# Moving weight and input loads between queues and visits in a fused attention and MLP kernel

## The chip, the cores and the metric

The kernel runs on one core of one Trainium2 chip. The metric is the device time of one execution in microseconds (us). Three timed runs of the kernel before took 363.74, 364.76 and 366.37 us; their median is 364.76. One further execution was taken with a profile.

## The reference, cut to what matters

One transformer block over 2048 tokens of width 576, in bfloat16, with a sliding, dilated attention (32 heads of 18, eight taps two tokens apart) and an MLP of width 4608:

```python
def A(x):                                   # x already normalised
    q, k, v = split(x @ wqkv)               # wqkv: 576 x 1728
    # token s sees s, s-2, ..., s-14 of its own head
    logits = einsum("bhsd,bhswd->bhsw", q, k[idx]) * 18 ** -0.5
    o = einsum("bhsw,bhswd->bhsd", softmax(masked(logits)), v[idx])
    return o @ wo                           # wo: 576 x 576
def B(y):
    return gelu(y @ w1 + b1) @ w2 + b2      # w1: 576 x 4608, w2: 4608 x 576
h   = x + A(layernorm(x))
out = h + B(layernorm(h))
```

## The kernel before

**Tiles.** Token `p * 16 + j` lies on partition `p` of tile `j`, so there are 16 tiles of 128 tokens. The taps of an even tile are even tiles. Even and odd tiles form two rings, and attention goes through each ring from the top down (`ATT_ORDER`); A[0] and A[1] below are its first two tiles, 14 and 12. A tap that would fall below tile 0 is a tile of the partition above. So, after a tile is done, its K or V slot in the ring is replaced by the same rows moved down one partition: `store_halo` writes K and V to DRAM (`kv_dram`), and `halo` reads them back shifted (`kv_ring<-kv_dram`).

**First stage.** TensorE (PE) computes Q, K and V in 24 visits, each of two products of one tile with one of the three weight blocks; a visit takes about 2.5 us. Visits 0 to 11 are for the even tiles, 12 to 23 for the odd ones, two tiles (three visits) at a time. The contraction of 576 rows is four blocks of 128 (`wq_sb`) and a tail of 64, held twice, once for each half of the array (`wqh_sb`, loaded in two parts r). Even tiles are turned by PE (`tr_x`). Odd tiles are normalised on ScalarE (ACT), stored to DRAM (`out_x`, `xd<-q_all`) and read back turned by a DMA transpose (`in_x`, `xnT<-xd`), two tiles in one transpose; the first is wanted at visit 12, the third at visit 18.

Between these visits VectorE (DVE) works through LN statistics of all tiles and the attention of A[0] and A[1]: product of K and Q (L340), sums (L349), softmax, product with V (L395), sums (L401, L402). The product of A[1] with V needs the V halo of A[0]. PE then turns A[1]'s result (`tr_o`, `o_pt`) into PSUM tile "D", which the addition of x (`ln2_h`, L459) of A[0] has to free first. Wo is first used at visit 17. `add_b2` (L501) adds b2, loaded by SP at visit 14, to A[0]'s sum.

**The MLP** follows in eight groups of two tiles: w1 is read as six column pieces of 768 KB in order (`load_w1(0)` to `load_w1(5)`), w2 in seven.

**What sets the order.** It is written out by hand: the text between `manual_schedule` and the loop, and the tables `after`, `between`, `hooks` and `loads`, which say what is issued after which visit. Each engine executes its instructions in that order. Loads go out on SP unless an engine is named, and SP takes them strictly in order: an issue that waits holds all behind it. Each weight load issued in the visits also waits for the last PSUM read-out of its visit (`pace`). [...]

Of the kernel before, what the change touches and what calls it, by code (L numbers as in the profile page):

```python
# [17 lines left out]
def kernel(  # L18
# [12 lines left out]
    nc = tc.nc  # L31
    P = 128
    _, S, D = A_x.shape
# [12 lines left out]
    HP = P // 2  # L46
# [7 lines left out]
    EVEN, ODD = QKV_ORDER[:NT // 2], QKV_ORDER[NT // 2:]  # L54
# [3 lines left out]
    x3 = A_x.rearrange("b (p j) d -> p (b j) d", j=NT)  # L58
# [12 lines left out]
    x_all = wpool.tile([P, NT, D], BF16, name="x_all")  # L71
# [18 lines left out]
    wqh_sb = qp.tile([P, 3, D], BF16, name="wqh_sb")  # L90
# [9 lines left out]

    pace = [None]

    def load(out, in_):
        ins = nc.sync.dma_start(out=out, in_=in_).ins
        if pace[0] is not None:
            tc.add_manual_dep(ins, pace[0].name, sync_dep, reason="pace of the weight loads")

    def load_x(js):
        j0, n, step = js[0], len(js), 2
        load(x_all[:, j0:j0 + step * (n - 1) + 1:step, :], x3[:, j0:j0 + step * (n - 1) + 1:step, :])  # L110

    def load_wqkv(t, k0=0, k1=KF):
        load(wq_sb[:, k0:k1, t * D:(t + 1) * D],
             A_wqkv[k0 * P:k1 * P, t * D:(t + 1) * D].rearrange("(k p) c -> p k c", p=P))

    def load_wqkv_half(engine, t0, t1, r):
        n = D if r else HALF
        engine.dma_start(out=wqh_sb[half_rows(r), t0:t1, 0:n],
                         in_=A_wqkv[D - P + r * HP:D - HP + r * HP, t0 * D:t1 * D].rearrange("p (t c) -> p t c", c=D)[:, :, 0:n])

    def load_wo(qs):
        src = A_wo.rearrange("(h d) c -> h d c", h=H)
        for q in qs:
            load(wo_sb[q * H:(q + 1) * H, :, :], src[:, q:4 * KF:4, :])
            load(woh_sb[q * H:(q + 1) * H, :], src[:, 4 * KF + q % 2, q // 2 * HALF:(q // 2 + 1) * HALF])
# [82 lines left out]
    def half_rows(r):  # L208
        return slice(r * HP, (r + 1) * HP)
# [468 lines left out]
    def c_(fn, *a):  # L678
        return lambda: fn(*a)
# [99 lines left out]

    with tc.manual_schedule(engines={ENG.PE, ENG.Activation, ENG.DVE, ENG.SP, ENG.Pool}):  # L780
        load_x(EVEN[0:1])
        load_x(EVEN[1:2])
        for r in range(2):
            load_wqkv_half(nc.scalar, 1, 3, r)
        load_wqkv(1, 0, 2)
        load_wqkv(1, 2, KF)
        load_x(EVEN[2:3])
        load_wqkv(2, 0, 2)
        load_wqkv(2, 2, KF)
# [5 lines left out]
        load_wqkv(0, 0, 2)  # L795
        load_wqkv(0, 2, KF)
        for r in range(2):
            load_wqkv_half(nc.sync, 0, 1, r)
        nc.vector.memset(prod[:, 0:2, :], 0.0)
        nc.sync.dma_start(out=kv_dram[:, 0, :, :], in_=prod[0:NT, 0:2, :])  # L800
        load_w1h()
# [2 lines left out]
        for n in [512] * 8 + [P] * 5:  # L804
            nc.tensor.matmul(busy[:, 0, 0:n], lhsT=ones[:, 0:P], rhs=ones[:, 0:n], start=True, stop=True)
        nc.gpsimd.memset(mhalf[:], -0.5)
        nc.gpsimd.memset(eps2[:], EPS * EPS)
        make_identity(nc, ident[:])
        ln1_groups = [EVEN[0:1], EVEN[1:2], EVEN[2:3], EVEN[3:4], EVEN[4:5], EVEN[5:6],
                      EVEN[6:7], EVEN[7:8], ODD[0:4], ODD[4:6], ODD[6:8]]  # L810
        ln1 = {}
# [93 lines left out]
            ln2_send(d)  # L905
            ln2_ins(c, d)

        loads = {v: [c_(load_w1, c)] for c, v in enumerate((2, 3, 11, 13, 15, 17))}
        loads[4] = [c_(load_wo, range(4))]
        for n, v in enumerate((19, 19, 20, 20, 21, 22)):  # L910
            loads[v] = loads.get(v, []) + [c_(load_w2, n)]
        after = {
# [84 lines left out]
        p, q, r, s = "ABDC"  # L997

        gelu_table()
        for k, g in enumerate(GROUPS):  # L1000
            c, d = GROUPS[k + 1] if k + 1 < len(GROUPS) else (None, None)
# [87 lines left out]
            if 3 <= k < 7:  # L1089
                mlp2_fast(g, rows, (s, p, q, r), wo, x, True)  # L1090
                p, q, r, s = q, r, p, s
            else:
                mlp2_fast(g, rows, (q, p, r, s), wo, x)
                p, q, r, s = r, s, p, q
# [30 lines left out]
```

## Time and profile before

| | us |
|---|---|
| timed runs, median (lowest, highest) | 364.76 (363.74, 366.37) |
| profiled execution: its time | 363.39 |
| profiled execution: its span | 361.6 |
| PE busy in the span | 354.1 |
| DVE busy | 296.1 |
| ACT busy | 234.6 |
| GpSimd (POOL) busy | 46.5 |
| share of 16 transfer engines, ordinary queue | 43.6% |
| granted TensorE clock | 0.999 |

A line of a timeline is start, length, engine and line, operation, tiles, count, and in brackets the idle time of the engine before it and what ended it. A line of the chain of waits is start, length and what the end of the kernel went back to; "DMA" there is the time from issue to landing. [...] SPq, ACTq and POOLq are issues by these engines' sequencers. The names `w_sb` and `b_sb` are `w1_sb` and `b1_sb`: the profile leaves numbers out.

### The profile page before, as it was taken

Reading aid. Unit: us, or ns where it says so; the run is one execution under the profiler, and the core shown is the slowest. Engines: PE = TensorE matmul, PEld = TensorE weight load, DVE = VectorE, ACT = ScalarE, POOL = GpSimd, SP = SyncE. Lnnn points to the kernel's source line nnn. Section 1 sums busy time; section 2 is a strip of 40 time slices with the busy share of each in tenths; the row PEclk is TensorE's granted clock in tenths of the full one; section 3 lists DMA queues with packets and bytes.
Section 4 is the critical chain, followed back from the end, with each engine's and each line's share of the span. In section 5 each row is a group of like instructions: output and inputs, shape, how many; then the busy total and the mean of one; then the engine's idle time right before and its main releaser. Section 6 shows DMA issues by size and latency. Waiting matters only on the chain.

```text
span 361.6 us, 11550 instructions
## 1 busy us (share of the span) xinstructions
PE 354.1 (98%) x4942; PEld 295.1 (82%) x4942; DVE 296.1 (82%) x414; ACT 234.6 (65%) x519; POOL 46.5 (13%) x61
## 2 busy tenths in 40 slices
PE   8999999999999999999999999999999999999996
PEld 4778977887779977887788778877887788779974
DVE  5999989999989998997799899989998997520431
ACT  3879755897646783668656956695669566606620
POOL 2241004000112020201110202021102100201000
PEclk9999999999999999999999999999999999999999
DMA  8976699972546595732464555444545254343001
GB/s 244 322 249 192 189 269 274 377 248 64 149 87 105 172 206 95 129 78 51 82 111 106 66 125 84 106 83 107 86 106 83 62 84 70 51 106 51 4 1 34
DMA packets 62916, 46.18 MB, mean 128 GB/s; under 512 B 32192, under 2 KB 60608, under 8 KB 62864
## 3 DMA queue, kind: packets, MB, share of 16 engines
q1 hardware_dynamic: 58896, 41.39, 43.6%
q0 software_dynamic: 3744, 3.84, 9.8%
q8 instruction: 38, 0.62, 0.8%
q10 hardware_dynamic: 224, 0.22, 0.3%
q14 instruction: 14, 0.11, 0.1%
HBM read 23.27 MB, written 12.42 MB: 99 GB/s over the span
## 4 chain that ended last, share of the span: by engine, by line
PE 64%; DVE 21%; DMA 7%; ACT 3%; issue 2%; SPq 2%; POOL 0%; POOLq 0%; DVEq 0%; ACTq 0%
PE pm L218 34%; PE po L666 21%; PE po L578 5%; DVE prod L349 4%; DVE prod L340 3%; PE pw L218 3%; DVE prod L395 3%; DVE ln_stats L150 3%; ACT h_all L559 2%; DVE prod L401 2%; DMA td<-hn 2%; DMA hnT<-td 2%; DMA kv_ring<-kv_dram 1%; DMA x_all<-in_A_x_dram 1%; PE pq L218 1%
## 5 line engine op out<-in xcount | busy, mean ns | idle before, releaser
L218 PE MATMUL pm<-hnT,w_sb 64*128 64x256 bf16 x2304 | 143.0, 269 | 1.0 <-DMA hnT<-td 1.0
L559 ACT ACTIVATE h_all<-pm,b_sb 128x256 f16<-128x256 f32 (+1 forms) x288 | 108.4, 495 | 52.2 <-PE pm L218 51.6
L218 PEld LDWEIGHTS <-w_sb 64*128 64x128 bf16 x2304 | 115.2, 94 | 12.8 <-issue 2.7
L666 PEld LDWEIGHTS <-h_all 128*128 128x128 f16 x480 | 46.2, 98 | 13.7 <-issue 1.6
L218 PE MATMUL pq<-wq_sb,xnT 64*128 64x288 bf16 x720 | 55.6, 287 | 0.8 <-ACT xnT L269 0.3
L218 PEld LDWEIGHTS <-xnT 64*128 64x128 bf16 x864 | 44.5, 95 | 10.0 <-ACT xnT L269 0.7
L349 DVE TENSOR_TENSOR prod<-prod 128x2304 bf16<-128x2304 bf16 (+1 forms) x64 | 44.2, 691 | 2.0
L340 DVE TENSOR_TENSOR prod<-kv_ring,q_all 128x4608 bf16<-128x4608 bf16 x16 | 40.9, 2555 | 3.2 <-POOL ln_rstd L479 2.4
L395 DVE TENSOR_TENSOR prod<-kv_ring,probs 128x4608 bf16<-128x4608 bf16 x16 | 40.9, 2558 | 1.6 <-DMA kv_ring<-kv_dram 1.0
L218 PE MATMUL pm<-hnT,w1h_sb 64*128 64x256 bf16 x288 | 39.8, 269 | 0.0
L666 PE MATMUL po<-w2a_sb,h_all 128*128 128x288 bf16 (+1 forms) x262 | 35.9, 286 | 0.0
L401 DVE TENSOR_TENSOR prod<-prod 128x2304 bf16<-128x2304 bf16 (+1 forms) x32 | 33.9, 1058 | 1.1
L578 PEld LDWEIGHTS <-h_all 128*128 128x128 bf16 x288 | 27.8, 98 | 7.9 <-issue 0.9
L666 PEld LDWEIGHTS <-kv_ring 128*128 128x128 f16 x252 | 24.6, 98 | 6.3
L578 PE MATMUL po<-w2a_sb,h_all 128*128 128x288 bf16 x224 | 28.5, 286 | 0.0
L218 PE MATMUL pq<-wqh_sb,xnT 64*128 64x288 bf16 x144 | 27.9, 287 | 0.0
L768 POOL DMA_DIRECT2D x_all<-o_sb x12 | 10.6, 887 | 125.1 <-PE pw L218 72.3
L646 DVE TENSOR_TENSOR kv_ring<-h_all 128x1536 f16<-128x1536 f16 (+3 forms) x9 | 6.8, 760 | 16.9 <-ACT h_all L559 16.9
L479 POOL TENSOR_TENSOR ln_rstd<-ln_var,mhalf 128x1 f32<-128x1 f32 x13 | 9.3, 717 | 81.9 <-ACT ln_var L478 81.9
L666 PE MATMUL po<-w2b_sb,h_all 128*128 128x288 bf16 (+1 forms) x122 | 19.7, 286 | 0.1
L163 POOL TENSOR_TENSOR ln_rstd<-ln_veps,mhalf 128x1 f32<-128x1 f32 (+2 forms) x14 | 13.4, 964 | 48.9 <-DVE ln_veps L157 32.3
L218 PE MATMUL pw<-wo_sb,oT 64*128 64x288 bf16 x256 | 19.5, 283 | 0.1
(107 smaller groups left out, 399.7 us busy)
## 6 DMA issues: line engine op xcount, KB each, us to landing
w_sb<-in_B_w_dram SPq DMA_DIRECT2D x6, 768.0 KB, 6.4
kv_ring<-kv_dram SPq DMA_DIRECT2D x28, 144.0 KB, 2.2
kv_dram<-kv_ring SPq DMA_DIRECT2D x13, 288.0 KB, 4.6
x_all<-in_B_b_dram SPq DMA_DIRECT2D x15, 144.0 KB, 4.2
w2a_sb<-in_B_w_dram SPq DMA_DIRECT2D x2, 1008.0 KB, 7.4
td<-q_all SPq DMA_DIRECT2D x14, 144.0 KB, 1.8
td<-hn SPq DMA_DIRECT2D x14, 144.0 KB, 1.8
x_all<-h POOLq DMA_DIRECT2D x14, 144.0 KB, 4.5
```

The costliest lines, as they stand in the source:

```text
L150: nc.vector.bn_stats(out=stats[:, i, c, :], in_=src[:, c * HALF:(c + 1) * HALF])
L163: nc.gpsimd.tensor_tensor(out=rstd[:], in0=veps[:], in1=mhalf[:].to_broadcast([P, n]), op=ALU.pow)
L218: last = nc.tensor.matmul(duo["g"][r ^ swap][i], lhsT=lhsT, rhs=rhs, start=(swap == 0 and i == 0 and kt == 0), stop=(swap == 1 and kt == K ...
L340: ins = nc.vector.tensor_tensor(out=prod[:], in0=k_ring[j % 2], in1=q_all[:, j, :].unsqueeze(1) .to_broadcast([P, W, D]), op=ALU.mult).ins
L349: nc.vector.tensor_tensor(out=prod[:, :, o * H:o * H + n], in0=prod[:, :, a * H:a * H + n], in1=prod[:, :, c * H:c * H + n], op=ALU.add)
L395: nc.vector.tensor_tensor(out=prod[:].rearrange("p w (d h) -> p w d h", h=H), in0=v_ring[j % 2].rearrange("p w (d h) -> p w d h", h=H), in ...
L401: nc.vector.tensor_tensor(out=prod[:, 0:n, :], in0=prod[:, 0:n, :], in1=prod[:, n:2 * n, :], op=ALU.add)
L479: ins = nc.gpsimd.tensor_tensor(out=rstd[:], in0=var[:], in1=mhalf[:], op=ALU.pow).ins
L559: pace[0] = nc.scalar.activation(out=hT(grp)[:, f, 0:N], in_=ps[:, r, i * N:(i + 1) * N], func=ACT.Gelu_apprx_tanh, bias=b1_sb[:, f:f + 1] ...
L578: nc.tensor.matmul(banks[half], lhsT=hT(grp)[:, f, i * P:(i + 1) * P], rhs=w2_rows(f)[:, half * HALF:(half + 1) * HALF], start=(f == 0), s ...
L666: nc.tensor.matmul(bank, lhsT=l, rhs=r, start=start, stop=stop, skip_group_check=True)
L768: nc.gpsimd.dma_start(out=x_of(j), in_=o_of.pop(j), accum_op=ALU.add)
```

## The change

The second x tile is issued by ACT and not by SP. The K tails, issued by ACT together with the V tails before, are issued by ACT alone, behind the x tile; the V tails are issued by GpSimd, behind the making of the identity. The third w1 piece is issued after visit 4, where Wo was, and not after visit 11. Wo, eight DMAs after visit 4 before, goes out in four parts of two DMAs after visits 6, 8, 11 and 12. The order of all other instructions on every engine stays as it was.

```diff
-    def load(out, in_):
-        ins = nc.sync.dma_start(out=out, in_=in_).ins
+    def load(out, in_, engine=nc.sync):
+        ins = engine.dma_start(out=out, in_=in_).ins
...
-    def load_x(js):
+    def load_x(js, engine=nc.sync):
         j0, n, step = js[0], len(js), 2
-        load(x_all[:, j0:j0 + step * (n - 1) + 1:step, :], x3[:, j0:j0 + step * (n - 1) + 1:step, :])
+        load(x_all[:, j0:j0 + step * (n - 1) + 1:step, :], x3[:, j0:j0 + step * (n - 1) + 1:step, :], engine)
...
-    def load_wqkv_half(engine, t0, t1, r):
+    def load_wqkv_half(engine, t, r):
         n = D if r else HALF
-        engine.dma_start(out=wqh_sb[half_rows(r), t0:t1, 0:n],
-                         in_=A_wqkv[D - P + r * HP:D - HP + r * HP, t0 * D:t1 * D].rearrange("p (t c) -> p t c", c=D)[:, :, 0:n])
+        engine.dma_start(out=wqh_sb[half_rows(r), t, 0:n], in_=A_wqkv[D - P + r * HP:D - HP + r * HP, t * D:t * D + n])
...
         load_x(EVEN[0:1])
-        load_x(EVEN[1:2])
-        for r in range(2):
-            load_wqkv_half(nc.scalar, 1, 3, r)
+        load_x(EVEN[1:2], nc.scalar)
         load_wqkv(1, 0, 2)
         load_wqkv(1, 2, KF)
+        for r in range(2):
+            load_wqkv_half(nc.scalar, 1, r)
         load_x(EVEN[2:3])
...
         for r in range(2):
-            load_wqkv_half(nc.sync, 0, 1, r)
+            load_wqkv_half(nc.sync, 0, r)
...
         make_identity(nc, ident[:])
+        for r in range(2):
+            load_wqkv_half(nc.gpsimd, 2, r)
...
-        loads = {v: [c_(load_w1, c)] for c, v in enumerate((2, 3, 11, 13, 15, 17))}
-        loads[4] = [c_(load_wo, range(4))]
+        loads = {v: [c_(load_w1, c)] for c, v in enumerate((2, 3, 4, 13, 15, 17))}
+        for q, v in enumerate((6, 8, 11, 12)):
+            loads[v] = [c_(load_wo, [q])]
```

## The prediction

> **What bounds the kernel now.** I read the page first, then the chain of waits up to 110 us, then the PE and weight-load timelines for idle time, the SP timeline, and last the DMA issues in narrow windows, for landings. The page: TensorE is busy nearly throughout.
>
> ```profile
> PE 354.1 (98%) x4942; PEld 295.1 (82%) x4942; DVE 296.1 (82%) x414; ACT 234.6 (65%) x519; POOL 46.5 (13%) x61
> PE 64%; DVE 21%; DMA 7%; ACT 3%; issue 2%; SPq 2%; POOL 0%; POOLq 0%; DVEq 0%; ACTq 0%
> ```
>
> So loads can only win idle PE time, about 7.5 us, of which 0.8 lies before the first matmul and 3.6 in the last 12 us. The other places are few. In the chain of waits the end runs through VectorE (DVE) up to 99 us, and back from there to the first loads:
>
> ```profile
> 0.74 3.52 DMA wqh_sb<-in_A_wqkv_dram
> 4.27 0.37 SPq L104
> ...
> 4.69 4.74 DMA x_all<-in_A_x_dram
> ...
> 9.45 0.83 DVE ln_stats L150 x2
> ```
>
> Read upwards: the statistics of the fourth even tile wait for its load; that load was issued late because the one before it on SP, the second V weight piece, stood until the K/V tail of ScalarE's queue (ACT) landed. The same chain in the window 40 to 70 us:
>
> ```profile
> 40.52 2.57 DVE prod L395
> 43.08 0.04 issue
> 43.12 4.96 DMA kv_ring<-kv_dram
> ...
> 48.18 2.57 DVE prod L395
> ...
> 53.41 0.68 DVE h L459
> 54.09 0.04 issue
> 54.13 0.47 PE o_pt L183 x12
> ```
>
> DVE waits for a halo read that takes 5.0 us (2.2 is its least in this stretch), and PE then waits for DVE. The timelines (start, length, what, idle time before it) give the price of this wait, what stands ahead of the halo on SP, and two waits for transposed x:
>
> ```profile
> 48.18 2.56 DVE L395 TENSOR_TENSOR prod<-kv_ring,probs 128x4608 bf16<-128x4608 bf16 x1 [1.00 <-DMA kv_ring<-kv_dram]
> 54.13 0.47 PE L183 MATMUL o_pt<-ident,q_all 64*128 64x64 bf16 x12 [0.87 <-DVE h L459]
> 41.78 1.29 SPq L104 DMA_DIRECT2D w_sb<-in_B_w_dram x1
> 43.12 0.50 SPq L335 DMA_DIRECT2D kv_ring<-kv_dram x1
> 36.00 1.09 PEld L218 LDWEIGHTS <-xnT 64*128 64x128 bf16 x20 [0.31 <-DMA xnT<-xd]
> 50.88 2.07 PEld L218 LDWEIGHTS <-xnT 64*128 64x128 bf16 x36 [0.26 <-DMA xnT<-xd]
> ```
>
> The 768 KB of w1 issued at 41.78 land 5.8 us later, at 47.6, and the halo at 48.1, just behind. That w1 piece is the one the change moves.
>
> **The change, part by part.** I count from this execution's own time, 363.39 us, a span of 361.6 and 1.8 around it.
>
> *Start.* The second x tile goes out on ACT at 0.74, where SP issued it at 1.20. All that SP issues behind it comes one issue earlier: 0.46 by the row. What waits for it: ACT's first activation, idle 1.34 until 4.79. ACT now issues three DMAs; two took 1.40, so three take about 2.1, the table load 1.28 follows, and ACT is ready near 4.2: the x tile's path may gain up to 0.6. [...] Value for the whole start: 0.4, nearest to the issue row; bounds 0 and 0.6, the DVE idle time before 9.45 (0.60), past which DVE's own earlier work binds. A loss I exclude: total bytes are the same, and the transfer engines are 0.60 busy in the first 5 us at 154 GB/s, against 363 GB/s in the next 5.
>
> [...]
>
> K tails: issued behind the x tile at about 1.4 and 2.1, landing by the tail row (3.9) at 6.0; first used at 7.71. V tails: two issues on GpSimd behind the identity (done at 1.4), 0.89 each by the accumulating stores' row, done at 3.2; its next work is at 6.12. Landing by the slowest GpSimd DMA row (4.5) at 7.7; first used at 10.71. Both cost nothing; without that cover each us late is a us of PE.
>
> *Halo.* After the change the halo has ahead of it one Wo part (144 and 18 KB) in place of 768 KB. The stores ahead of that landed at 45.4 and 45.6 (5.2 and 4.9 after issue); two transfers of some 0.4 each at 363 GB/s put the halo at about 46.5. DVE is ready at 47.18 (46.76 and 0.42). So its 1.00 idle goes and the product starts at 47.21: minus 0.97; bounds 0.97 and 0.
>
> *PE behind it.* PE was ready for o_pt 0.87 earlier, at 53.26, and 0.26 of what it did before was the wait at 50.88, which has 768 KB less ahead of it. So PE can follow DVE by all 0.97.
>
> *Third w1 piece early.* It is now issued at 21.55, directly behind pieces 0 and 1 (landed at 22.7 and 26.2) and one store, where Wo had 648 KB. Two w1 pieces issued back to back at 54.06 and 54.55 landed 2.8 apart, pieces 0 and 1 3.5: so it lands at about 29.3 to 30.0, where the last Wo part landed at 28.7. Behind it are the halo of 27.56 (landed 29.75; DVE needs it at 31.98: cover 2.2) and the store of x that the first transpose waits for (landed 30.4). That transpose ends PE's wait at 36.0, so its delay is PE's delay: 0 to 0.6; value 0.2, since the transfer engines were only 0.36 busy from 26 to 28. It eats PE's 0.26 and not DVE's gain.
>
> *Wo parts.* Removed from SP: eight issues between 21.55 and 27.02. Added, two issues (0.87) each: part 0 in SP's idle time for the stored x (28.93 to 30.79), part 1 in the one before the next halo (35.28 to 36.57), part 2 in place of the w1 issue of 1.29, part 3 between the halo and the next transpose (43.62 to 45.66). All fit: no cost. The last part lands near 47.0, and Wo is first used at 48.56: cover 1.5, less the 0.4 of the start. If it took 5.8 us like the w1 piece there, PE would stand 0.9.
>
> *What is late next.* DVE's add of b2 starts at 57.96, and the b2 load (issued 52.88, 5.0 to land) landed at 57.9; the product before it ended at 57.84. So DVE's gain ends here unless b2 comes earlier. Its issue follows the last transpose on SP, which waits for a store; all of these share the queue from which 444 KB go (768 less twice 162), 1.25 us at 363 GB/s. If b2 moves by the start alone, DVE gives back 0.97 less 0.12: 0.85; if by all, nothing. Value 0.3, since transposes and waits stand between as well as bytes.
>
> *Sum.* 0.4 + 0.97 - 0.3 = 1.07 on DVE; PE 0.4 + 0.87 + 0.26 - 0.2 = 1.33, of which DVE's wait for hnT at 106.7 leaves 1.07. From there PE runs alone and only shifts. 363.39 - 1.07 = 362.3. The three timed runs have a median of 364.76 (363.74 to 366.37), all above the profiled one; the median of all four is 364.25, and from it the forecast is 363.2.
>
> **Rivals.** *Given back:* b2 and the first transpose take most of it, the start is worth only its issue. For it: the two rows above with covers of 0.12 and 0. Against: the queue carries less. Gain 0.3: 364.0. *Slower:* the third w1 piece, at SP's queue 21.55, holds back the store of x and with it the first transpose. If it took the 6.3 us of piece 0 after piece 1 landed, it would land at 32.5, the halo at 32.9 in place of 29.75, and PE would stand at visit 12 3.15 longer; less 1.13 (the waits of 0.87 and 0.26) and 0.4 is 1.6 slower: 365.0 by its own time, 365.9 by the four runs. It decides from a delay of 1.5. Against: the spacings of 2.8 and 3.5. *More:* every PE wait of the stretch goes (0.24 at 25.4, 0.29, 0.26, 0.87, 0.16 at 62.1) and the start gives 0.6: 2.4, so 361.8. Against: b2.
>
> **How the numbers follow.** Forecast (gain 0.6 to 1.6) 0.55, given back 0.22, slower 0.12, more 0.11. The range takes the slower case's price, the larger gain, and some 0.4 for where a median falls among runs that differ by 2.6: 361.4 to 365.9. One per cent, about what a measurement of this kernel can tell from no change, is 3.6 us: no case reaches it alone, so within it 0.88; faster needs the largest gain and low runs, 0.08; slower needs w1 later still or a tail late, 0.04.
>
> **What would show it.** DVE's wait at 48.2 gone and the halo's landing near 3.4 us; PE's wait for o_pt at most 0.2; the statistics of 9.45 starting near 9.0; the wait at visit 12 at most 0.5. Wrong if a w1 piece takes over 8 us to land at 21.6, if PE waits for woh or wo tiles at visit 17, or if DVE stands before the add of b2 for over 0.8.

## The result

The changed kernel takes 363.1 us in the median of 22 runs (362.34 to 364.53), the kernel before 364.06 in 22 runs beside them: a ratio of 0.9972 with a 95% interval of 0.9959 to 0.9985, so 1.0 us less. Two later comparisons of the same two kernels gave 0.9994 (0.9973 to 1.0015) and 0.9980 (0.9961 to 0.9999). Weighted by their intervals the three give 0.9979, some 0.8 us. The forecast was 363.2, a gain of 1.07.

The profiled execution of the changed kernel took 364.12 us, 0.7 more than the profiled one of before (363.39), though its median is lower. So a single pair of profiles misleads here, and most readings below are made on several executions.

The page of the changed kernel, busy times and the engines' shares of the chain that ended last:

```profile
PE 353.4 (98%) x4942; PEld 294.0 (81%) x4942; DVE 295.9 (82%) x414; ACT 234.8 (65%) x519; POOL 47.7 (13%) x63
...
PE 71%; DVE 14%; DMA 9%; ACT 2%; issue 2%; SPq 1%; POOL 0%; DVEq 0%; POOLq 0%; ACTq 0%
```

VectorE's (DVE's) part of the chain has fallen from 21% to 14%. Its first part, in the window 0 to 16 us, answers to the first chain shown of before (start, length, what; the changed kernel's line numbers are one lower up to about L780 and one higher at L823):

```profile
0.74 3.12 DMA x_all<-in_A_x_dram
3.86 0.02 issue
3.88 0.37 SPq L104
4.25 0.04 issue
4.29 5.53 DMA x_all<-in_A_x_dram
9.81 0.02 issue
9.84 0.83 DVE ln_stats L149 x2
```

SP no longer waits for a tail at 4.27 but for the second x tile, until 3.88, and the load of the fourth even tile goes out at 4.29 instead of 4.69. But it takes 5.53 us instead of 4.74, and the statistics start at 9.84, not at 9.0: the start has lost 0.39. Around the halo (the chain in the window 40 to 70 us):

```profile
43.79 0.11 SPq L104
43.94 0.43 SPq L104
44.47 3.17 DMA kv_ring<-kv_dram
47.73 2.57 DVE prod L394
50.33 1.37 DVE prod L400
51.72 0.77 DVE prod L400
52.51 0.46 DVE q_all L401
52.97 0.68 DVE h L458
53.69 0.47 PE o_pt L182 x12
```

The halo read takes 3.17 us instead of 4.96, and the product behind it starts 0.45 earlier although DVE came 0.37 later. The timelines of the same execution show what is left of the two waits:

```profile
47.73 2.56 DVE L394 TENSOR_TENSOR prod<-kv_ring,probs 128x4608 bf16<-128x4608 bf16 x1 [0.19 <-DMA kv_ring<-kv_dram]
...
57.31 0.75 DVE L500 TENSOR_TENSOR x_all<-h,x_all 128x576 bf16<-128x576 f32 x1
```
```profile
53.69 0.47 PE L182 MATMUL o_pt<-ident,q_all 64*128 64x64 bf16 x12
```

DVE's 1.00 is 0.19, TensorE's (PE's) 0.87 for `o_pt` is gone, and the add of b2 starts 0.65 before that of the kernel before, with no wait. From there DVE and PE run some 0.7 ahead up to 292 us (the wait for `hnT` near 106 ends at 105.99 instead of 106.71). Then this execution lost 1.4 us:

```profile
306.74 0.66 PE L217 MATMUL pw<-wo_sb,oT 64*128 64x288 bf16 x8 [0.59 <-DMA oT<-td]
325.44 0.61 PE L217 MATMUL pm<-hnT,w_sb 64*128 64x256 bf16 x8 [1.39 <-DMA hnT<-td]
```

The kernel before had no wait at the first place in its profile, and 0.71 at the second. Whether the change does this was a question for the further profiles.

### The profile page after: what moved, and what is told of

Its sections match the earlier page's. It is cut to its first block, busy times and chain, and to the rows that moved or that the text cites. A ratio compares the mean times of both kernels' runs of the same rounds, so it can differ in the third digit from the quotient of the medians.

```text
span 362.4 us, 11559 instructions
## 1 busy us (share of the span) xinstructions
PE 353.4 (98%) x4942; PEld 294.0 (81%) x4942; DVE 295.9 (82%) x414; ACT 234.8 (65%) x519; POOL 47.7 (13%) x63
## 4 chain that ended last, share of the span: by engine, by line
PE 71%; DVE 14%; DMA 9%; ACT 2%; issue 2%; SPq 1%; POOL 0%; DVEq 0%; POOLq 0%; ACTq 0%
PE pm L217 33%; PE po L665 24%; PE pq L217 5%; PE po L577 5%; PE pw L217 4%; DVE ln_stats L149 2%; DMA x_all<-in_A_x_dram 2%; DVE prod L394 2%; DMA kv_ring<-kv_dram 2%; DVE prod L348 2%; DMA hnT<-td 2%; DVE prod L339 1%; DMA oT<-td 1%; DVE prod L400 1%; ACT h_all L558 1%
## 5 line engine op out<-in xcount | busy, mean ns | idle before, releaser
L217 PE MATMUL pq<-wq_sb,xnT 64*128 64x288 bf16 x720 | 54.6, 283 | 1.3 <-DMA wq_sb<-in_A_wqkv_dram 0.6
```

The lines of the kernel that those rows point to most:

```text
L217: last = nc.tensor.matmul(duo["g"][r ^ swap][i], lhsT=lhsT, rhs=rhs, start=(swap == 0 and i == 0 and kt == 0), stop=(swap == 1 and kt == K ...
```

## The experiments

Theory A, from the two traces: the start loses 0.4 and the loads win 1.2. Theory B, the forecast: the start wins 0.4 and the loads 0.7. Theory C: waits behind 290 us, not these, decide the time. Each comparison of times is with runs of the kernel before beside it. A gain in us below is that of the ratio; the medians alone can give another (for the fourth x tile ahead of V 1.0 in place of 1.6).

**Loads alone.** Start of before, w1 and Wo as in the change:

```diff
-        loads = {v: [c_(load_w1, c)] for c, v in enumerate((2, 3, 11, 13, 15, 17))}
-        loads[4] = [c_(load_wo, range(4))]
+        loads = {v: [c_(load_w1, c)] for c, v in enumerate((2, 3, 4, 13, 15, 17))}
+        for q, v in enumerate((6, 8, 11, 12)):
+            loads[v] = [c_(load_wo, [q])]
```

> The kernel before with the second half of the change alone: third w1 piece at visit 4, the four Wo parts at visits 6, 8, 11 and 12; the start stays as it was. Theory A, from the two traces (the start lost 0.4 us on VectorE, the loads won 0.8 at the halo and 0.25 at b2): this kernel is the best of the parts, 1.2 to 1.4 us below the kernel before, so below the whole change; the statistics of the fourth even tile start at 9.45 as before, the product that follows the 43 us halo starts near 47.2. Theory B, the forecast (the start wins 0.4, the loads 0.7): 0.7 below the kernel before, so above the whole change. Theory C (what is seen before 290 us doesn't decide, waits behind 290 us do): no order between this kernel, the start alone and the whole change.

Measured: 363.99 (12 runs) against 364.81, ratio 0.9982 (0.9964 to 0.9999), 0.66 us. DVE has no wait at the halo (product at 47.44) and none at b2. The statistics came at 9.67, later than expected. The time fits theory B's 0.7; with an interval of 0.04 to 1.3 us it doesn't exclude A's 1.2.

**Start alone.** The other half of the change, on the loads of before (the diff of the change without its last block).

> The kernel before with the first half of the change alone: second x tile and K tails on ScalarE's queue, V tails on GpSimd's; loads of w1 and Wo as they were. Theory A: the statistics of the fourth even tile start near 9.84, 0.4 late; 0 to 0.4 us above the kernel before. Theory B: they start near 9.0, 0.4 below the kernel before. Theory C: within 0.2 of the kernel before.

Measured: 364.59 against 364.81, ratio 1.0002 (0.9980 to 1.0025). The statistics start at 9.81: theory B's 9.0 is refuted. Something else appears, in PE's timeline (first fence) and in the table of stretches of the same kernel (second fence: stretch, its length, busy time of PE, PEld, DVE, ACT, POOL with counts, granted clock, busy share of the transfer engines, GB/s):

```profile
6.07 0.42 PE L217 MATMUL pq<-wq_sb,xnT 64*128 64x288 bf16 x4 [0.19 <-ACT xnT L268]
7.33 0.67 PE L217 MATMUL pq<-wq_sb,xnT 64*128 64x288 bf16 x4 [0.84 <-DMA wq_sb<-in_A_wqkv_dram]
```
```profile
7.00:8.00 1.00, 0.67 (x6) 0.48 (x7) 0.29 (x1) 0.00 (x0) 0.00 (x0) 0.50 1.08 345
8.00:9.00 1.00, 1.00 (x12) 0.74 (x10) 0.93 (x4) 0.00 (x0) 0.00 (x0) 0.50 1.09 360
9.00:10.00 1.00, 1.00 (x12) 0.74 (x10) 0.36 (x2) 0.00 (x0) 0.00 (x0) 0.50 1.07 392
10.00:11.00 1.00, 1.00 (x16) 0.82 (x14) 0.93 (x4) 0.50 (x1) 0.00 (x0) 0.79 1.05 389
```

PE begins its first product early, then waits 0.84 for the second K weight piece, and around that wait its granted clock is 0.50 for 3.4 us (three whole rows, and 0.42 of the next by its mean of 0.79): four products take 0.67 instead of the 0.42 of the line before. The halo wait is there as before (1.33).

**No loads on GpSimd.** The changed kernel, both tails in two transfers again, on ScalarE's (ACT's) queue behind the x tile:

```diff
         load_wqkv(1, 2, KF)
         for r in range(2):
-            load_wqkv_half(nc.scalar, 1, r)
+            load_wqkv_half(nc.scalar, 1, 3, r)
...
-        for r in range(2):
-            load_wqkv_half(nc.gpsimd, 2, r)
```

> The changed kernel, but the K and V tails go in the same two transfers as before, on ScalarE's queue behind the second x tile; GpSimd issues none. If the small packets of GpSimd's two transfers (146 to 318 ns each, between 4.25 and 6.5 us) are what delayed the third and fourth even x tiles: their landing comes back to 9.4 or earlier, the statistics start between 9.0 and 9.45, and the kernel is 0.4 to 0.8 below the changed one. If it is that the first two x tiles, issued at the same moment, share the transfer engines (first x tile landed 0.72 later), or that SP's loads are issued behind one another anyway: statistics stay near 9.8 and the time is within 0.2 of the changed kernel.

Measured: 364.54 against 364.81, ratio 0.9997 (0.9977 to 1.0017). Neither expectation: the statistics are later still, at 10.48, and PE waits 1.70 for the K piece. So GpSimd's packets aren't needed for the delay. What is common to this kernel and the change is that the second x tile goes out on ACT, and that tails move when the transfer engines are full (busy share 1.03 and 1.05 from 2.5 to 4.5 and 4.5 to 7.5 us in this kernel); no run moves the one without the other. The same kind of table, before first and then the changed kernel:

```profile
0.00:2.50 2.50, 1.72 (x5) 0.64 (x6) 0.54 (x1) 0.33 (x1) 0.77 (x8) 1.00 0.25 59
2.50:4.50 2.00, 2.00 (x9) 0.88 (x8) 1.40 (x4) 0.95 (x1) 0.00 (x0) 1.00 0.94 239
4.50:7.50 3.00, 2.00 (x32) 1.11 (x32) 1.43 (x5) 2.28 (x6) 1.11 (x2) 1.00 1.06 343
```
```profile
0.00:2.50 2.50, 1.72 (x5) 0.64 (x6) 0.54 (x1) 0.11 (x1) 1.74 (x10) 1.00 0.20 31
2.50:4.50 2.00, 2.00 (x9) 0.88 (x8) 0.81 (x2) 1.79 (x3) 0.28 (x1) 1.00 1.05 353
4.50:7.50 3.00, 1.86 (x33) 1.11 (x32) 1.91 (x7) 1.78 (x6) 1.09 (x2) 1.00 1.06 295
```

The last two columns are the ones to read. From 2.5 us on the transfer engines are full in both (0.94 to 1.06). Before moves its tails first (72 and 144 KB, 3.5 and 3.9 us from issue to landing, where the first x tile's 144 KB took 2.2), at 239 GB/s, and then x and weights at 343; the changed kernel has a head start at 353 and pays at 295. The bytes up to 7.5 us are the same: 59 x 2.5 + 239 x 2 + 343 x 3 = 1655 KB against 31 x 2.5 + 353 x 2 + 295 x 3 = 1669. No time is won by the order of these bytes, and the tails of the change now move among what DVE and PE wait for (they landed at 4.9, 6.9, 7.3 and 7.5). With equal sums the third even x tile landed at 7.36 and 7.73. What makes the difference can't be read from these sums over 16 engines. This stays open.

**Third w1 piece behind the halo.** The kernel before with one number changed:

```diff
-        loads = {v: [c_(load_w1, c)] for c, v in enumerate((2, 3, 11, 13, 15, 17))}
+        loads = {v: [c_(load_w1, c)] for c, v in enumerate((2, 3, 12, 13, 15, 17))}
```

> The kernel before with one number changed: the third w1 piece is issued at visit 12 in place of 11, so behind the V halo of the first odd tile instead of ahead of it; Wo stays at visit 4. If the 768 KB ahead of the halo are the whole of the gain: VectorE's wait of 1.00 at 48.2 and the tensor engine's of 0.87 for o_pt go, and 0.8 to 1.2 us are won. Rival, that the bytes only move to the next wait: the w1 piece now stands ahead of the next transpose of xn, TensorE's wait at 50.9 (0.26) grows to 1 or more, and under 0.4 us are won.

Measured: 363.82 against 364.81, ratio 0.9978 (0.9957 to 0.9999), 0.8 us. The halo wait and that for `o_pt` are gone, and the weight loads' wait for the third transpose grew from 0.26 to 0.60, not to 1 (PE itself stood 0.29 there); but DVE's timeline shows the gain handed back two instructions later, and not at the place that the rival named:

```profile
47.19 2.56 DVE L395 TENSOR_TENSOR prod<-kv_ring,probs 128x4608 bf16<-128x4608 bf16 x1
...
57.90 0.76 DVE L501 TENSOR_TENSOR x_all<-h,x_all 128x576 bf16<-128x576 f32 x1 [1.06 <-DMA x_all<-in_B_b_dram]
```

**The same, with b2 ahead.** b2 is issued before the fourth transpose, which waits until the store of its tiles has landed (2.8 us in the first profile of before):

```diff
-            14: [c_(att_pv, A[1]), c_(in_x, 3), c_(load, b2_bc, B_b2.partition_broadcast(P))],
+            14: [c_(att_pv, A[1]), c_(load, b2_bc, B_b2.partition_broadcast(P)), c_(in_x, 3)],
```

> The kernel before with two edits: the third w1 piece at visit 12, behind the V halo, and at visit 14 the load of b2 issued ahead of the fourth transpose of xn instead of behind it (about 52.2 in place of 53.5). In the kernel with the first edit alone VectorE won the halo's 1.00 and stood 1.06 for b2 at 57.9. If b2 is what gave it back: b2 lands near 56.6, the wait of 1.06 goes, the add of b2 starts near 56.9, 1.0 earlier than with the first edit alone, and the time is 0.6 to 1.0 below that kernel's. If the next wait takes it anyway (the fourth transpose lands later, TensorE waits for it at visit 22): the add starts early, but TensorE is no earlier at 62, and the time is within 0.3 of the first edit's.

Measured: 363.02 against 363.78, ratio 0.9967 (0.9951 to 0.9982), 1.2 us below before, 0.4 more than with the first edit alone; the intervals overlap. The wait of 1.06 is gone and the add starts at 56.67, 1.23 earlier. b2 was issued at 50.33 instead of 53.47.

**Fourth x tile ahead of V.** Loads of the change, start of before, and:

```diff
+        load_x(EVEN[3:4])
         load_wqkv(2, 0, 2)
         load_wqkv(2, 2, KF)
-        load_x(EVEN[3:4])
```

> The loads of the change on the start of before (the kernel with the loads alone), and the fourth even x tile issued ahead of the two V weight pieces instead of behind them; nothing is put on another engine. If the landing of the x tiles is what sets VectorE up to 48 us: its 0.63 of idle time before the statistics of that tile goes, all that follows on VectorE is 0.5 to 0.6 earlier than in the kernel with the loads alone, and the time 0.3 to 0.6 lower. If the V pieces, now some 0.4 later, are as close: TensorE waits for them instead and the time stays.

Measured: 362.74 (9 runs) against 363.78, ratio 0.9956 (0.9933 to 0.9979). DVE's wait moves one tile on:

```profile
8.73 0.81 DVE L150 BATCH_NORM_STATS2 ln_stats<-x_all 128x6 f32<-128x288 bf16 x2
10.81 0.82 DVE L150 BATCH_NORM_STATS2 ln_stats<-x_all 128x6 f32<-128x288 bf16 x2 [0.61 <-DMA x_all<-in_A_x_dram]
```

The fifth tile starts at 10.81; with the loads alone it was 11.05, in the first profile of before 10.83. So the 0.5 to 0.6 did not come. PE waited 0.21 and 0.38 for V pieces. That the time is nevertheless 1.6 below before (1.0 by the medians) isn't explained by these rows; its interval overlaps that of the loads alone.

**Both kernels again.**

> The kernel before once more, unchanged, for a second profile and for what the comparison says of no change: ratio 1.000 within 0.002. If the waits behind 290 us scatter from one execution to the next, its wait for the transposed h near 325 is 0.9 to 1.4 in place of 0.71, and the span above 361.6; the wait of 1.00 for the halo at 48.2 and that of 0.87 for o_pt at 54.1 must be there again (0.8 to 1.2).

Measured: 364.06 against 363.78, ratio 0.9997 (0.9981 to 1.0012). The wait for `hnT` is 1.22 and that for `o_pt` 0.95. The halo wait, expected at up to 1.2, is 2.13: the piece of 768 KB was issued at 42.67, landed at 48.58, and the halo at 48.99.

> The changed kernel once more, unchanged, beside the same runs of before: 0.7 to 1.1 us below. Its second profile has the statistics of the fourth even tile at 9.8 again (by the forecast, 9.0), no wait of VectorE above 0.3 at the halo of 47.7 nor at the add of b2; the waits at 306 (0.59) and 325 (1.39) of its first profile differ if they are scatter, and are there again if the change makes them.

Measured: 364.02 against 363.78, ratio 0.9994 (0.9973 to 1.0015): less gain than expected. The statistics start at 9.49, the halo costs nothing, and the wait at 306 is not there, so that one was scatter; at 325 it is 1.29. But now b2 is late (DVE's timeline):

```profile
47.22 2.56 DVE L394 TENSOR_TENSOR prod<-kv_ring,probs 128x4608 bf16<-128x4608 bf16 x1
...
57.78 0.76 DVE L500 TENSOR_TENSOR x_all<-h,x_all 128x576 bf16<-128x576 f32 x1 [0.90 <-DMA x_all<-in_B_b_dram]
```

DVE was half a microsecond further than in the first profile and lost it all: the prediction's rival "given back", in this execution. It had been no part of the first.

**Loads with b2 ahead; the whole change with b2 ahead; x tile and b2 ahead.** The edits above put together: the first is the loads alone, the second the change, the third the loads with the fourth x tile ahead of V, each with b2 ahead of the transpose. The changed kernel ran with them a third time.

> The kernel with the loads of the change alone (start of before), and b2 issued ahead of the fourth transpose of xn at visit 14. VectorE's wait for b2 was 0, 0, 0.20 and 0.90 in four executions with these loads. If that wait is what makes the gain come and go: no wait at the add of b2, and 0.2 to 0.4 below the loads alone in the mean, so 1.0 to 1.4 below the kernel before; the span of the runs is narrower. If it is not: the same as the loads alone, 0.8 below before.

Measured: 362.78 against 364.84, ratio 0.9945 (0.9927 to 0.9963), 2.0 us below before, more than expected. No wait at the halo or at b2; the runs lie in 362.10 to 363.78, those with the loads alone in 362.80 to 365.51. The interval lies below that of the loads alone (0.9964 to 0.9999), so the one place is worth something by itself, 1.3 us by the two ratios; that is more than the waits for b2 in the profiles with these loads (0 to 0.20 with the start of before) explain.

> The whole change, and b2 issued ahead of the fourth transpose of xn. Beside the run of the loads with b2 ahead it differs by the start alone, with no wait for b2 to hide it. If the start costs what the statistics of the fourth even tile show (9.46 to 9.84 against 9.20 to 9.67): 0.2 to 0.4 slower than the loads with b2 ahead, 0.6 to 1.0 below the kernel before. If the start is worth its issue (the forecast's 0.4): 0.4 faster.

Measured: 363.43, ratio 0.9961 (0.9942 to 0.9980). It is 0.65 slower than the loads with b2 ahead, on the side of the start's cost; but the two intervals overlap (from 0.9942 to 0.9963). Statistics at 9.93, PE's wait for the K piece 0.93, and the granted clock at 0.50 from 8 to 10 us.

> The loads of the change, the fourth even x tile ahead of the V pieces, b2 ahead of the fourth transpose, nothing on GpSimd's queue. The wait for the fifth tile (0.61) took most of what the fourth gave, 0.2 were left on VectorE. If those add up: 0.1 to 0.3 below the loads with b2 ahead, 1.2 to 1.6 below before, and the lowest of all. If TensorE's waits for the V pieces (0.21 and 0.38) cost as much: the same as the loads with b2 ahead.

Measured: 362.37 (6 runs, 361.94 to 362.77), ratio 0.9935 (0.9909 to 0.9961), 2.4 us below before, the lowest median of all. DVE's timeline, which is ahead of every other kernel's at each of these places:

```profile
8.57 0.82 DVE L150 BATCH_NORM_STATS2 ln_stats<-x_all 128x6 f32<-128x288 bf16 x2
10.01 0.82 DVE L150 BATCH_NORM_STATS2 ln_stats<-x_all 128x6 f32<-128x288 bf16 x2
...
55.99 0.75 DVE L501 TENSOR_TENSOR x_all<-h,x_all 128x576 bf16<-128x576 f32 x1
```

This time there is no wait at 10. That it beats the loads with b2 ahead (362.78) is within their intervals.

> The changed kernel unchanged, a third profile and the base for the kernel with b2 ahead in the same call: 0.4 to 1.0 below before. VectorE waits for b2 between 0 and 0.9, at the halo of 47.7 between 0 and 0.3; the statistics of the fourth even tile between 9.4 and 9.9.

Measured: 364.12 (362.24 to 365.16), ratio 0.9980 (0.9961 to 0.9999), as expected; 11 of its 12 runs are above the slowest of the six of the kernel before it in this list. Its profiled execution is its slowest, and goes far past the expected bounds: statistics at 10.52, and, on PE and DVE:

```profile
6.17 0.66 PE L217 MATMUL pq<-wq_sb,xnT 64*128 64x288 bf16 x4 [0.19 <-ACT xnT L268]
7.90 0.66 PE L217 MATMUL pq<-wq_sb,xnT 64*128 64x288 bf16 x4 [1.07 <-DMA wq_sb<-in_A_wqkv_dram]
```
```profile
48.29 2.56 DVE L394 TENSOR_TENSOR prod<-kv_ring,probs 128x4608 bf16<-128x4608 bf16 x1
59.52 0.76 DVE L500 TENSOR_TENSOR x_all<-h,x_all 128x576 bf16<-128x576 f32 x1 [1.58 <-DMA x_all<-in_B_b_dram]
```

PE is late from the start here, and SP is ever later behind the first profile: 0.7 at the first transpose (31.98 for 31.27), 1.0 at the third (47.08 for 46.06), 1.6 at the fourth (53.60 for 51.98). b2 behind it goes out at 55.07 and lands at 59.50, and DVE, only 0.6 late, stands. SP's timeline of the first profile of before (first fence), what SP waited for in it from 42 to 54 us (second: us in total, times, longest), and SP's timeline of this one (third):

```profile
51.55 1.29 SPq L282 DMA_TRANSPOSE xnT<-xd  x1
52.88 0.58 SPq L104 DMA_DIRECT2D x_all<-in_B_b_dram  x1
```
```profile
SPq L282 <- DMA xd<-q_all: 4.7, 2, 2.8
...
SPq L282 <- PE pq L218: 1.3, 1, 1.3
```
```profile
53.60 1.34 SPq L281 DMA_TRANSPOSE xnT<-xd  x1
55.07 0.50 SPq L104 DMA_DIRECT2D x_all<-in_B_b_dram  x1
```

What holds the fourth transpose is the store of its tiles (`xd<-q_all`), 2.8 us there and 3.4 here. The 1.3 put down to PE is no wait: the issue of a transpose takes that long at all four places (1.29 to 1.46 in the first profile of before), and none of the 32 transposes in the first profile of either kernel is issued in less than 1.2. That PE's delay at 8 us is what comes back as DVE's wait at 58 isn't shown.

All profiled executions together (us; "K piece" is PE's wait for the second K weight piece near 7, "statistics" the start for the fourth even tile, the last two are waits of DVE):

| kernel | ratio | statistics | K piece | halo | b2 |
|---|---|---|---|---|---|
| before, twice | 0.9997 | 9.45, 9.24 | 0, 0.16 | 1.00, 2.13 | 0, 0 |
| changed, three times | 0.9972, 0.9994, 0.9980 | 9.84, 9.49, 10.52 | 0.61, 0.27, 1.07 | 0.19, 0, 0 | 0, 0.90, 1.58 |
| start alone | 1.0002 | 9.81 | 0.84 | 1.33 | 0 |
| loads alone | 0.9982 | 9.67 | 0.28 | 0 | 0 |
| no loads on GpSimd | 0.9997 | 10.48 | 1.70 | 0.16 | 0.86 |
| w1 piece behind the halo | 0.9978 | 9.41 | 0.41 | 0 | 1.06 |
| the same, b2 ahead | 0.9967 | 9.16 | 0 | 0.22 | 0 |
| x tile ahead | 0.9956 | 8.73 | 0.28 | 0 | 0.20 |
| loads, b2 ahead | 0.9945 | 9.39 | 0 | 0 | 0 |
| change, b2 ahead | 0.9961 | 9.93 | 0.93 | 0 | 0 |
| x tile and b2 ahead | 0.9935 | 8.57 | 0.29 | 0 | 0 |

## Why the prediction was right, and where its steps were not

The time came out at the forecast (363.1 against 363.2), and the sign held in three comparisons, in the second within its interval of no change. Three of the steps were wrong, and that did not show in the sum of the first comparison. Of the prediction's own signs, "the statistics of 9.45 starting near 9.0" did not come, and "if DVE stands before the add of b2 for over 0.8" was met in two of three executions.

**Start: the sign was wrong.** The step that failed is "A loss I exclude: total bytes are the same, and the transfer engines are 0.60 busy in the first 5 us". The mean of 0.60 hid two stretches: up to 2.5 us almost nothing moves (0.25, 0.20), and from then on the engines are full (0.94 to 1.06). The bytes were indeed the same, but the free room lies ahead of the first landing (near 2.9 before, near 3.7 in the change). Five executions with the start of the change have the statistics at 9.92 in the mean (9.49 to 10.52), six with the start and order of before at 9.39 (9.16 to 9.67): 0.53 lost, where 0.4 was to be won. PE waits 0.74 for the K piece in the mean of the five, 0.14 in the six. In time the loss is at the edge of what the runs resolve: 0.65 between the two kernels with b2 ahead, 0.0 for the start alone. The load at 4.29 was issued 0.40 sooner (4.69 before) and landed 0.39 later (9.81 for 9.42): what the issue saved was lost on the way to the landing.

That K and V tails "cost nothing" was too sure. The second K tail landed at 7.5, 6.9 and 8.5 in the three profiles, not at 6.0: the cover was gone, and the product that needs it starts at the landing in two of them (7.57 and 8.52). SP, whose next x load goes out right behind that landing (7.54 in the first profile), stood 1.6, 1.0 and 2.3 us for it; no later wait shows a cost of that. No engine waited for a V tail.

**Halo: right.** DVE's 1.00 is 0.19, 0 and 0 in three executions, and the read takes 3.2 us or less against the forecast of 3.4. What was not counted is that SP came to the halo 1.35 us later (44.47 for 43.12), held by the stores and the Wo part ahead of it; so it landed at 47.64 and not near 46.5, and that is the 0.19 of the first profile. The wait itself was undersized: 1.00, 2.13 and 1.33 in three executions with the loads of before. Moving the w1 piece alone removes it too (0, and 0.22 with b2 ahead).

**PE behind it: mostly right.** The wait for `o_pt` is gone in all three. The 0.26 for the third transpose was to go; it is 0.42, 0.38 and 0.49.

**Third w1 piece: cheaper than forecast.** It was issued at 21.93 and landed at 27.74, not 29.3 to 30.0 (26.2 and 2.8 to 3.5 make 29.0 to 29.7); 27.6 and 28.9 in the other two. The first transpose landed at 35.68 (35.95 before); PE's wait at visit 12 is nothing, 0.50 and nothing. The rival "slower" had no ground. **Wo: right**; PE had no wait for it at visit 17.

**b2: the mechanism was right, the size was not.** The term is "Value 0.3, since transposes and waits stand between as well as bytes"; three executions show 0, 0.90 and 1.58. The bound of 0.85 named with it was about their mean. The step counted on b2 coming sooner because the queue carries less. It came out later, though its read got shorter (5.0 us, then 3.8 to 4.4): it was issued at 52.88 in the first profile of before, and at 53.42, 53.91 and 55.07 in the three of the changed kernel. It stands behind the fourth transpose, and that behind a store, as the prediction says; SP waited 2.8 us for this store in the first profile of before and 2.8, 3.4 and 3.4 in the three. In the second profile DVE had meanwhile won most, in the third SP was the latest. The four kernels with b2 ahead of that transpose wait for it 0; of the seven profiles with the w1 piece moved and b2 behind, five wait (0.20 to 1.58). So this order decides whether the gain is kept. Why SP's stores take longer in some executions stays open.

**"From there PE runs alone and only shifts" was wrong of single executions.** PE's wait ahead of the product with `hnT` near 325 us is between 0.67 and 1.39 in the 14 profiles (in that of the loads alone, 0.94, the profile puts it down to DVE), without order by kernel (before 0.71 and 1.22, changed 1.39, 1.29 and 0.95). At 306 us two of the 14 show 0.59 and 0.67 more, one of them a kernel with the start of before. So theory C holds for the difference between two profiles; nothing shows it for that between the medians.

The terms as measured do not add up closely: start +0.5, halo -1.4 (1.49 in the mean before, 0.06 after), b2 +0.8 give about -0.1, and the runs about -0.8. Three profiles, one of them the slowest of its kernel's runs, are too few for more; which runs had a late b2 can't be seen from their times. The agreement of the first comparison with the forecast is thus in part luck.

## What to carry to other kernels

Before moving loads to other queues, split the busy share of the transfer engines into short stretches: here a mean of 0.60 hid that they stood at 0.94 to 1.06 from 2.5 us on, and with an x tile and tails on other queues the load issued 0.40 sooner landed 0.39 later. When a wait goes, look at the next load that the same engine needs and at what its issue stands behind; if that waits itself, as the transpose here for a store (2.8 to 3.4 us), the gain lasts only as long as that wait ends in time. A load issued one place earlier, with nothing else changed, may be what keeps it (b2 here: no wait in four profiles, up to 1.58 us where it was issued behind). And before a name in a list of waits is believed, see whether the same instruction takes as long where it has nothing to wait for (a transpose's issue here, 1.29 to 1.46 us at all four places).

## What was not expected of the hardware

PE's granted clock fell to 0.50 around waits of 0.84, 0.93 and 1.70 us near 7 to 8 us (start alone, change with b2 ahead, no loads on GpSimd), each time for about 3.4 us by the rows' means: 0.50, 0.50, 0.50, 0.79 from 7 to 11 us, 0.60, 0.50, 0.50, 0.69 from 7 to 11, and 0.87, 0.50, 0.50, 0.50, 0.93 from 8 to 13. PE was also only partly busy in the 3 us from 4 to 7 (1.35, 1.45 and 1.90 us of them), and the runs don't show what brought the slow clock.

The granted clock of the rows isn't the whole truth for the first microseconds: in the third profile of the changed kernel the rows give 1.00 while four products take 0.66 us at 6.17 and again at 7.90, as long as under a clock of 0.50 in the start alone (0.67), where 0.42 is usual; only 12 or 13 matmuls stand in each us from 9 to 13. The first profile of before has the same, with the start of before and no wait for a K piece (same columns as the tables above):

```profile
7.00:8.00 1.00, 1.00 (x12) 0.57 (x10) 1.00 (x3) 0.10 (x1) 0.29 (x1) 1.00 1.09 357
8.00:9.00 1.00, 1.00 (x12) 0.63 (x10) 0.78 (x3) 0.00 (x0) 0.00 (x0) 1.00 1.10 364
```

There are 12 matmuls in each of these, as in the rows at 0.50 of the start alone; its second profile has 22 and 21. So the slow pace comes without the change and without that wait too, and the 0 for the K piece in this profile's row is in part that PE came to it late.

Loads with the same sum of bytes ahead of them by 7.5 us (29 x 2.5 + 354 x 2 + 295 x 3 = 1666 KB in the third profile, 1669 in the first) landed 0.93 us apart: the third even x tile at 8.66 and at 7.73, in two executions of the same kernel.
